# One-bank sums in the input phase and a new order of block products in the output phase of a fused attention and two-expert kernel

## The chip, the cores and the metric

The kernel runs on one core of one Trainium2 chip. The metric is the device time of one execution in microseconds (us); a lower time is better.

## The reference

Causal local attention with a few global keys feeds two dense blocks one after the other. The part that matters here is the last block, on 3072 tokens:

```python
x = _moe_ref(x=x, ...)          # (a * b @ w3) @ w_out, d_model 512
h = x @ w_in                    # 512 -> 2048
g = h * np.cos(h)
return (g @ w_out).astype(np.float32)   # 2048 -> 512
```

## The kernel before

Attention and the first block take the first 616 us of the span and are the same before and after. What follows handles the last block. The 3072 tokens go in three rounds (q = 0, 1, 2) of 1024, each in two blocks of 512 columns. A round has an input phase (h = x @ w_in, and g = h cos h) and an output phase (g @ w_out).

Both phases use a scheme with seven block products in place of eight. Every product of fp32 matrices is made of three fp32r matmuls (`mm3`, L419): each operand is split into a high part and a low remainder, and high x high, high x low and low x high are summed in a PSUM bank.

**Input phase** (`phase_a`, L1141, called for k = 0 to 7): one call makes a pair of 128-row blocks of h, as tiles `jj` and `gg` of 128x1024. It issues seven products (`prod`, L1065) of six matmuls each, in the order 0 to 6 of the list `PRODS`, so 42 matmuls of 128x512. They go to four sums a, b, c, d: product 0 starts a, 1 starts b, 2 starts c, 3 starts d, then 4 is added to a, 5 to c, 6 to d. In between, the sums are read as partial results: ACT copies a (`s1`, L1162), VectorE (DVE) makes `s` = b + s1, `v` = c + s (written to tile `vv`), and `gg`'s second half = d + v (all L1152); once 4, 5 and 6 have been added, ACT copies a into `jj` (L1188), and DVE writes c + s to `gg` and d + s to `jj`. Before the change a and b are the two halves of one PSUM tile of two banks, and c and d those of another (`two_banks`, L1062), from a ring of four such tiles, which is the whole PSUM.

A **gate** (class `Gate`, L1081) turns a finished tile h of 128x1024 into h cos h: `turns` (ACT, L1088, into a two-bank PSUM tile of integers), two fused multiply-adds (DVE, `rest_steps`, L1097), absolute value (`size`, ACT, L1103), sine (`cosine`, ACT, L1106), multiply (`times`, GpSimd, here POOL, L1111). The gates of k - 1 are spread over the call for k, the tail of g0 over the call after that.

**Output phase** (`phase_b`, L1265): 56 steps, seven products times eight pairs k, in an order written out as the list `turn` (L1113). A step makes six matmuls, three into each of two banks. Its moving operand `op` is split by `op_split` (L1208): a copy to fp32r on ACT (L1214), a subtraction on DVE (L1215), three steps ahead of its use. Operands of products 1, 2, 3 and 6 are first made by `fold` (L1223), a subtraction, on POOL for 2 and 3 and on DVE for 1 and 6. The gates of pair 7 and the tail of those of pair 6 run inside the first steps (`last_gates`, L1235), since the input phase ends with pair 7. `evict` (L1287) adds finished sums up and sends them out.

Every engine runs its instructions in the order in which the code issues them. Weights come as `piece` tiles of 512 KB, loaded by the SP queue in the order of use (`pieces_to`, L1125) into a ring of eight; a load waits until the tile that it takes over has been read. `op` tiles rotate over two slots of tag `op` and four of tag `Wb`; the gates' work tiles `r` use `Wb` too. Remainders of the next round's input operands (`x2_steps`) run on ACT and DVE from step 16 on and in the first call of the next input phase. In round 0 three small steps of `needs_general` (L721) take turns with the steps of the output phase.

Of the kernel before, what the change touches and what calls it, by code (L numbers as in the profile page):

```python
# [271 lines left out]
def fused(ctx, tc, a_qk, a_v, a_v0, w3p, wo1p, w1p, w2p, winp, wo2p, out):  # L272
# [448 lines left out]
    def needs_general(nv, psum):  # L721

        misc.tile([128, 88], F32, name="fill_f")
        f = misc.tile([128, 4], F32, name="flags")
        nl, ng = nv[:, 0:1], nv[:, 1:2]
        nc.vector.tensor_reduce(
            out=f[:, 0:1], in_=top.rearrange("p a b -> p (a b)"), axis=AXIS.X, op=ALU.max
        )
        nc.vector.tensor_scalar(f[:, 0:1], f[:, 0:1], -0.9 * NEG, None, ALU.is_ge)
        nc.vector.tensor_scalar(f[:, 1:2], nl, 1.0, None, ALU.is_lt)  # L730
        nc.vector.tensor_scalar(f[:, 2:3], nl, float(LOC + 1), None, ALU.is_gt)
        nc.vector.tensor_scalar(f[:, 3:4], ng, float(GLB), None, ALU.is_gt)
        yield
        t = psum()[:, 0, :]
        nc.tensor.transpose(t[0:4, 0:128], f, ident)
        m = misc.tile([4, 128], F32, name="flag_rows")
        nc.vector.tensor_copy(out=m, in_=t[0:4, 0:128])
        c = misc.tile([4, 1], F32, name="flag_col")
        nc.vector.tensor_reduce(out=c, in_=m, axis=AXIS.X, op=ALU.max)
        yield  # L740
        nc.tensor.transpose(t[0:1, 128:132], c, ident[0:4, 0:4])
        r = misc.tile([1, 4], F32, name="flag_row")
        nc.vector.tensor_copy(out=r, in_=t[0:1, 128:132])
        flag = misc.tile([1, 1], F32, name="flag")
        nc.vector.tensor_reduce(out=flag, in_=r, axis=AXIS.X, op=ALU.max)
        flag_i = misc.tile([1, 1], I32, name="flag_i")
        nc.vector.tensor_copy(out=flag_i, in_=flag)
        yield flag_i

    with tc.manual_schedule():  # L750
# [309 lines left out]
        banks = {}  # L1060

        def two_banks(dt=F32):  # L1062
            return p_h.tile([128, 2, TB2], dt, tag="h", name="h_ps")

        def prod(q, k, i):  # L1065

            bank, name = PRODS[i]
            if i in (0, 2):
                t = two_banks()
                banks["ab" if i == 0 else "cd"] = t  # L1070
                for e in range(2):
                    banks["abcd"[i + e]] = t[:, e, :]
            n, half = divmod(7 * k + i, 2)
            w, x = pieces[q, n][:, half], x2c[name]
            mm3(
                banks[bank],
                [(w[:, e, 0, :], w[:, e, 1, :], x[:, e, 0, :], x[:, e, 1, :]) for e in range(2)],
                i < 4, True, i >= 4,
            )
# [34 lines left out]
        for prods, ks in (  # L1114
            ((0,), range(NP - 1)), ((2,), range(NP - 3)), ((0,), (NP - 1,)),
            ((2,), range(NP - 3, NP)), ((4, 1, 3, 5, 6), range(NP)),
        ):
            turn += [(i, k) for i in prods for k in ks]
# [22 lines left out]
        def phase_a(q, k, x2_last):  # L1141
# [27 lines left out]
            if k:  # L1169
                fold(3, k - 1)  # L1170
            if k > 1:
                fold(2, k - 2)
            prod(q, k, 2)
# [16 lines left out]
            add(gg[:, 0, :], banks["c"], s)  # L1190
            if k == NP - 1:
                for n in range(3):
                    op_split(0, n)
            g1[k].turns()
            add(jj[:, 1, :], banks["d"], s)

        t3 = {}
# [9 lines left out]

        def op_split(i, k):  # L1208
            at = op_count[0] % 6
# [4 lines left out]
            nc.scalar.copy(out=t[:, 0, :], in_=x)  # L1214
            nc.vector.tensor_tensor(  # L1215
                out=t[:, 1, :], in0=x, in1=t[:, 0, :].bitcast(F32), op=ALU.subtract
# [3 lines left out]

        def fold(i, k):

# [8 lines left out]
            }[i]  # L1231
            engine = nc.gpsimd if i in (2, 3) else nc.vector
            engine.tensor_tensor(out=out, in0=p, in1=q, op=ALU.subtract)  # L1233

        def last_gates():  # L1235
# [5 lines left out]
            a, b = g1[k].rest_steps(homes[0]), g0[k].rest_steps(homes[1])  # L1241
            next(a)
            g0[k - 1].cosine()
            g0[k - 1].times()
            yield
            next(a)
            g0[k].turns()
            fold(2, k - 1)
            yield
            next(b)  # L1250
            g1[k].size()
            g1[k].cosine()
            g1[k].times()
            yield
            next(b)
            yield
            g0[k].size()
            g0[k].cosine()
            g0[k].times()
            yield  # L1260
            fold(3, k)
            fold(2, k)
            yield

        def phase_b(q):  # L1265
# [21 lines left out]
            def evict(n):  # L1287

                p = ps[PRODS[n][0]]
                if n == 0:  # L1290
                    nc.scalar.copy(out=sv, in_=p)
                elif n == 2:
                    total(wv, p, sv)
                elif n == 4:
                    o = raw()
                    nc.scalar.copy(out=o, in_=p)
                    nc.sync.dma_start(out=place(0, 0), in_=o)
                elif n == 1:
                    total(sv, p, sv)
                    total(wv, p, wv)  # L1300
                elif n == 3:
                    total(wv, p, wv)
                    nc.sync.dma_start(out=place(1, 1), in_=wv)
                elif n == 5:
                    o = raw()
                    total(o, p, sv)
                    nc.sync.dma_start(out=place(0, 1), in_=o)
                elif not final:
                    total(sv, p, sv)
                    nc.sync.dma_start(out=place(1, 0), in_=sv)  # L1310

            def evict_last(i):

                for h, queue_ in enumerate((nc.scalar, nc.sync)):
                    c = slice(h * 256, h * 256 + 256)
                    total(sv[:, i, c], ps["d"][:, i, c], sv[:, i, c])
                    queue_.dma_start(out=place(1, 0)[:, i, c], in_=sv[:, i, c])

            def step(n, k, which):
# [3 lines left out]
                for i in which:  # L1323
                    if k == 0 and n < 4 and i == 0:
                        ps[bank] = two_banks()
                    mm3(
                        ps[bank][:, i, :],
                        [(w[:, i, 0, :], w[:, i, 1, :], x[:, 0, :], x[:, 1, :])],
# [3 lines left out]
            for at, (n, k) in enumerate(turn):  # L1332
                pieces_to(base + pairs_of.index((n, k // 2)) + 6)
                if at + 3 < len(turn):
                    op_split(*turn[at + 3])
                some(gates, 1)
                if at == 8 and not final:
                    x2_loads(q + 1)
# [5 lines left out]
                    x2_next = x2_steps(r0, r1)  # L1344
                for i, lag in ((1, 13), (6, 29)):
                    if 0 <= at - lag < NP:
                        fold(i, at - lag)
                if x2_next and at >= 16 and at % 3 == 0:
                    some(x2_next, 1)
                if q == 0 and at in (26, 30, 34):  # L1350
                    flags_of[0] = next(steps_f)
# [11 lines left out]

        steps_f = needs_general(nv, two_banks)
        flags_of = [None]
# [4 lines left out]
        flag = flags_of[0]  # L1370
        for p in (p_h, p2, late, x2cA, wts, edge):
            p.release()
# [85 lines left out]
```

## Time and profile before

| what | before |
|---|---|
| median of 3 runs (lowest to highest) | 1150.86 us (1150.82 to 1151.83) |
| the profiled execution: its own time, its span | 1149.4 us, 1147.2 us |
| PE matmul busy | 1087.0 us (95%) |
| DVE busy | 846.7 us (74%) |
| ACT busy | 728.3 us (63%) |
| POOL busy | 258.4 us (23%) |
| chain that ended last, by engine | PE 76%, DVE 15%, ACT 4% |

The span runs from the first to the last instruction that the profile shows, and 2.2 us of the execution lie around it. PE is the matrix engine and PEld its weight loads, which overlap the matmuls. A matmul's recorded duration contains the depth of the pipeline, so a row's duration is longer than the time until the next one starts; the pace is read from the starts. A bracket at the end of a timeline row is the engine's idle time before it and what ended that.

### The profile page before, as it was taken

The numbers are of one execution on the slowest core, as the hardware profiler recorded it, in microseconds if no ns is written. First come the engines' busy times: TensorE is split into PE (matmuls) and PEld (weight loads), VectorE is DVE, ScalarE is ACT, GpSimd is POOL, SyncE is SP. The second block draws the span as 40 slices with busy tenths as digits, with TensorE's granted clock in tenths as the row PEclk, the third lists the DMA queues.
The fourth block names the chain that finished last, engine by engine and source line by source line (L and its number), as shares of the span: only waits on it lengthen the run. The fifth ranks groups of instructions, "written<-read, shape, count | busy, mean of one in ns | idle before, by whom it ended". The sixth has DMA issues, their size and how long they took to land.

```text
span 1147.2 us, 17759 instructions
## 1 busy us (share of the span) xinstructions
PE 1087.0 (95%) x5922; PEld 928.3 (81%) x5922; DVE 846.7 (74%) x1807; ACT 728.3 (63%) x1475; POOL 258.4 (23%) x255
## 2 busy tenths in 40 slices
PE   8999999999999999999999888999898899988897
PEld 4557999999999999999998676777676687766585
DVE  8887768788687877878363677795767896777783
ACT  8988867676676776767332676463666553667541
POOL 0000011111121111112000666100566200466200
PEclk9999999999999999999999999899999999999999
DMA  9855466665766665674524455557554647545452
GB/s 334 277 180 170 146 206 200 223 211 186 233 201 227 206 218 194 208 229 138 187 98 138 165 176 174 182 193 265 168 164 163 211 174 275 170 164 164 144 183 95
DMA packets 88309, 219.25 MB, mean 191 GB/s; under 512 B 9488, under 2 KB 26384, under 8 KB 88208
## 3 DMA queue, kind: packets, MB, share of 16 engines
q1 hardware_dynamic: 87696, 217.44, 57.1%
q8 instruction: 49, 0.80, 0.3%
q10 hardware_dynamic: 512, 0.58, 0.2%
q14 instruction: 52, 0.43, 0.1%
HBM read 176.04 MB, written 41.94 MB: 190 GB/s over the span
## 4 chain that ended last, share of the span: by engine, by line
PE 76%; DVE 15%; ACT 4%; issue 2%; DMA 1%; POOL 0%; DVEq 0%; ACTq 0%; POOLq 0%; SPq 0%
PE h_ps L419 32%; PE mm L419 32%; DVE op L1215 3%; PE x_ps L644 3%; DVE r L1097 3%; PE mm L869 3%; PE pt_ps L617 2%; DVE gr L1152 1%; PE s_ps L559 1%; PE s_ps L555 1%; PE pt_ps L619 1%; ACT e L608 1%; DVE jj L1233 1%; PE s_ps L547 1%; ACT r L1103 1%
## 5 line engine op out<-in xcount | busy, mean ns | idle before, releaser
L419 PE MATMUL h_ps<-op,piece 128*128 128x512 f32 x1008 | 241.6, 398 | 20.3 <-DVE op L1215 16.1
L419 PEld LDWEIGHTS h_ps<-op,piece 128*128 128x128 f32 x1008 | 190.2, 191 | 70.6 <-DVE op L1215 24.8
L610 POOL TENSOR_SCALAR e<-e,st 128x232 f32<-128x232 f32 x148 | 77.0, 533 | 475.6 <-DVE st L602 388.7
L419 PE MATMUL mm<-xT,wA 128*128 128x384 f32 x768 | 146.7, 340 | 0.5 <-ACT xT L658 0.4
L419 PE MATMUL mm<-xT,wB 128*128 128x384 f32 x768 | 146.2, 339 | 0.0
L419 PE MATMUL mm<-ab,W 128*128 128x384 f32 x768 | 146.2, 340 | 0.0
L419 PE MATMUL h_ps<-B,piece 128*128 128x512 f32 x432 | 113.4, 397 | 26.6 <-DVE gr L1152 24.7
L419 PE MATMUL h_ps<-T,piece 128*128 128x512 f32 x576 | 138.4, 389 | 0.0
L419 PEld LDWEIGHTS mm<-xT,wA 128*128 128x128 f32 x768 | 130.9, 188 | 3.2 <-issue 1.8
L419 PEld LDWEIGHTS mm<-ab,W 128*128 128x128 f32 x768 | 131.1, 188 | 2.4 <-issue 2.4
L419 PEld LDWEIGHTS mm<-xT,wB 128*128 128x128 f32 x768 | 130.9, 188 | 2.1 <-issue 2.1
L419 PEld LDWEIGHTS h_ps<-T,piece 128*128 128x128 f32 x576 | 108.1, 188 | 22.7
L419 PEld LDWEIGHTS h_ps<-B,piece 128*128 128x128 f32 x432 | 79.1, 188 | 52.9 <-DVE gr L1152 33.6
L1111 POOL TENSOR_TENSOR gr<-r,gr 128x1024 f32<-128x1024 f32 x24 | 57.0, 2376 | 275.7 <-ACT r L1106 189.7
L589 ACT ACTIVATE e<-e,top 128x232 f32<-128x232 f32 (+1 forms) x192 | 89.3, 468 | 2.0 <-DVE top L578 2.0
L522 ACT CAST hh<-qk 128x720 fp32r<-128x720 f32 x74 | 58.9, 796 | 45.8 <-PE s_ps L559 43.1
L1103 ACT ACTIVATE r<-r 128x1024 f32<-128x1024 f32 x48 | 51.0, 1062 | 52.8 <-DVE r L1097 52.4
L578 DVE CUSTOM_DVE_ANT_0 e<-s_ps,bias 128x232 f32<-128x232 f32 (+1 forms) x192 | 65.0, 374 | 14.6 <-PE s_ps L559 9.7
L1111 POOL TENSOR_TENSOR jj<-r,jj 128x1024 f32<-128x1024 f32 x24 | 58.1, 2423 | 62.4 <-ACT r L1106 62.4
L1215 DVE TENSOR_TENSOR op<-jj,op 128x512 fp32r<-128x512 f32 x72 | 56.9, 810 | 14.8 <-ACT op L1214 14.8
L1215 DVE TENSOR_TENSOR op<-gr,op 128x512 fp32r<-128x512 f32 x72 | 57.6, 845 | 10.6 <-ACT op L1214 10.5
L869 PE MATMUL mm<-wo,w 128*128 128x512 f32 x128 | 61.2, 606 | 1.7 <-DVE wo L360 1.7
(129 smaller groups left out, 1860.8 us busy)
## 6 DMA issues: line engine op xcount, KB each, us to landing
piece<-a_s SPq DMA_DIRECT2D x84, 512.0 KB, 3.3
piece<-o2s SPq DMA_DIRECT2D x84, 512.0 KB, 3.3
qk<-in_a_qk SPq DMA_DIRECT2D x74, 360.0 KB, 3.4
a_s<-ap SPq DMA_DIRECT2D x56, 256.0 KB, 2.5
o2s<-ap SPq DMA_DIRECT2D x56, 256.0 KB, 2.4
v<-in_a_v SPq DMA_DIRECT2D x95, 128.0 KB, 3.3
raw<-in_w3p SPq DMA_DIRECT2D x16, 512.0 KB, 5.1
raw<-in_winp SPq DMA_DIRECT2D x16, 512.0 KB, 3.6
```

The costliest lines, as they stand in the source:

```text
L419: nc.tensor.matmul(ps, lhsT=l, rhs=r, start=first and i + e == 0, stop=last and i == n - 1 and e == 2, skip_group_check=more,)
L522: nc.scalar.copy(out=hh[n], in_=qk_raw[n])
L578: nc.vector.tensor_tensor_reduce(out=es[n][:, e, :w], in0=sp[:, e, :w], in1=bias[:, 2 * p + e, :], scale=-0.125, scalar=3.0e38, op0=ALU.ad ...
L589: nc.scalar.activation(es[n][:, e, :w], es[n][:, e, :w], ACTF.Exp, bias=top[:, n, e:e + 1], scale=-1.0, accum_out=sts[n][:, 0, e:e + 1],)
L610: nc.gpsimd.tensor_scalar(x, x, st[:, 1, e:e + 1], 1.0, ALU.mult, ALU.mult)
L617: nc.tensor.transpose(pt_ps[:, e, 0, :], e_t[:, e, :128], ident)
L644: nc.tensor.matmul(x[e * 64:(e + 1) * 64, i * 128:(i + 1) * 128], lhsT=vt[:kk, c, e * 64:(e + 1) * 64], rhs=pt[:kk, e, c, :], start=c == 0 ...
L869: nc.tensor.matmul(W_ps[m], lhsT=wt["w3", c][:, m * 128:(m + 1) * 128], rhs=wt["wo1", k], start=k == 0, stop=k == M1 - 1,)
L1097: nc.vector.scalar_tensor_tensor(out=self.r, in0=self.kt, scalar=-c, in1=x, op0=ALU.mult, op1=ALU.add)
L1103: nc.scalar.activation(self.r, self.r, ACTF.Abs)
L1111: nc.gpsimd.tensor_tensor(out=self.h, in0=self.r, in1=self.h, op=ALU.mult)
L1215: nc.vector.tensor_tensor(out=t[:, 1, :], in0=x, in1=t[:, 0, :].bitcast(F32), op=ALU.subtract)
```

## The change

The four sums of the input phase become four tiles of one bank each (pool `p_h`, four banks), and the remaining four banks are two tiles of two banks (pool `p_k`) for the gates' integers and for the output phase's sums b and c; its sums a and d take two one-bank tiles each. The output phase begins with products 0, 3 and 2 over pairs 0 to 6, then does pair 7 of these three, then products 4, 1, 5, 6 over all pairs; before it was product 0 over pairs 0 to 6, product 2 over 0 to 4, pair 7 of product 0, the rest of product 2, then 4, 1, 3, 5, 6. Operands are split four steps ahead instead of three; those of steps 0 and 1 are split during the calls for k = 6 and k = 7, with the subtraction on POOL, and those of steps 2 and 3 at the end of the call for k = 7. The last three folds of products 2 and 3 move from POOL to DVE, at steps 8, 10 and 12. The steps of `last_gates` are grouped anew. `evict` handles sums a and d by halves, and sum d is added when product 1 is done.

```diff
@@ -731,7 +731,7 @@
         nc.vector.tensor_scalar(f[:, 2:3], nl, float(LOC + 1), None, ALU.is_gt)
         nc.vector.tensor_scalar(f[:, 3:4], ng, float(GLB), None, ALU.is_gt)
         yield
-        t = psum()[:, 0, :]
+        t = psum()
         nc.tensor.transpose(t[0:4, 0:128], f, ident)
         m = misc.tile([4, 128], F32, name="flag_rows")
         nc.vector.tensor_copy(out=m, in_=t[0:4, 0:128])
@@ -1059,17 +1059,19 @@
         p_h = pool("p_h", 4, space=PSUM)
         banks = {}
 
+        p_k = pool("p_k", 2, space=PSUM)
+
+        def one_bank():
+            return p_h.tile([128, TB2], F32, tag="h", name="h_ps")
+
         def two_banks(dt=F32):
-            return p_h.tile([128, 2, TB2], dt, tag="h", name="h_ps")
+            return p_k.tile([128, 2, TB2], dt, tag="k", name="k_ps")
 
         def prod(q, k, i):
 
             bank, name = PRODS[i]
-            if i in (0, 2):
-                t = two_banks()
-                banks["ab" if i == 0 else "cd"] = t
-                for e in range(2):
-                    banks["abcd"[i + e]] = t[:, e, :]
+            if i < 4:
+                banks[bank] = one_bank()
...
@@ -1112,8 +1114,8 @@
 
         turn = []
         for prods, ks in (
-            ((0,), range(NP - 1)), ((2,), range(NP - 3)), ((0,), (NP - 1,)),
-            ((2,), range(NP - 3, NP)), ((4, 1, 3, 5, 6), range(NP)),
+            ((0, 3, 2), range(NP - 1)), ((0, 3, 2), range(NP - 1, NP)),
+            ((4, 1, 5, 6), range(NP)),
         ):
             turn += [(i, k) for i in prods for k in ks]
         pairs_of = list(dict.fromkeys((i, k // 2) for i, k in turn))
@@ -1167,9 +1169,11 @@
             gate(g1, k - 1, "cosine")
             gate(g1, k - 1, "times")
             if k:
-                fold(3, k - 1)
+                fold(3, k - 1, nc.gpsimd)
             if k > 1:
-                fold(2, k - 2)
+                fold(2, k - 2, nc.gpsimd)
+            if k >= NP - 2:
+                op_split(0, k - NP + 2, nc.gpsimd)
             prod(q, k, 2)
             prod(q, k, 3)
             some(x2_last, 2)
@@ -1188,11 +1192,11 @@
             nc.scalar.copy(out=jj[:, 0, :], in_=banks["a"])
             gate(g0, k - 1, "size")
             add(gg[:, 0, :], banks["c"], s)
-            if k == NP - 1:
-                for n in range(3):
-                    op_split(0, n)
             g1[k].turns()
             add(jj[:, 1, :], banks["d"], s)
+            if k == NP - 1:
+                op_split(0, 2)
+                op_split(0, 3)
 
         t3 = {}
 
@@ -1205,20 +1209,20 @@
 
         ops, op_count = {}, [0]
 
-        def op_split(i, k):
+        def op_split(i, k, engine=nc.vector):
             at = op_count[0] % 6
             op_count[0] += 1
             p, kw = (p2, {"tag": "op", "bufs": 2}) if at < 2 else (wts, {"tag": "Wb", "bufs": 4})
             t = ops[i, k] = p.tile([128, 2, TB2], F32R, name="op", **kw)
             x = raw_of(i, k)
             nc.scalar.copy(out=t[:, 0, :], in_=x)
-            nc.vector.tensor_tensor(
+            engine.tensor_tensor(
                 out=t[:, 1, :], in0=x, in1=t[:, 0, :].bitcast(F32), op=ALU.subtract
             )
 
         t3_two = {}
 
-        def fold(i, k):
+        def fold(i, k, engine=nc.vector):
 
             if i == 3:
                 if k % 2 == 0:
@@ -1229,7 +1233,6 @@
                 3: (t3.get(k), t[5], t[2]), 2: (t[2], t[2], t[0]),
                 1: (t[2], t[5], t[2]), 6: (t[4], t[4], t[2]),
             }[i]
-            engine = nc.gpsimd if i in (2, 3) else nc.vector
             engine.tensor_tensor(out=out, in0=p, in1=q, op=ALU.subtract)
 
         def last_gates():
@@ -1240,26 +1243,21 @@
             ]
             a, b = g1[k].rest_steps(homes[0]), g0[k].rest_steps(homes[1])
             next(a)
+            next(a)
             g0[k - 1].cosine()
             g0[k - 1].times()
             yield
-            next(a)
             g0[k].turns()
-            fold(2, k - 1)
-            yield
-            next(b)
             g1[k].size()
             g1[k].cosine()
             g1[k].times()
             yield
+            yield
             next(b)
-            yield
+            next(b)
             g0[k].size()
             g0[k].cosine()
             g0[k].times()
-            yield
-            fold(3, k)
-            fold(2, k)
             yield
 
         def phase_b(q):
@@ -1288,32 +1286,35 @@
 
                 p = ps[PRODS[n][0]]
                 if n == 0:
-                    nc.scalar.copy(out=sv, in_=p)
+                    for i in range(2):
+                        nc.scalar.copy(out=sv[:, i, :], in_=p[i])
                 elif n == 2:
                     total(wv, p, sv)
                 elif n == 4:
                     o = raw()
-                    nc.scalar.copy(out=o, in_=p)
+                    for i in range(2):
+                        nc.scalar.copy(out=o[:, i, :], in_=p[i])
                     nc.sync.dma_start(out=place(0, 0), in_=o)
                 elif n == 1:
                     total(sv, p, sv)
                     total(wv, p, wv)
-                elif n == 3:
-                    total(wv, p, wv)
+                    for i in range(2):
+                        total(wv[:, i, :], ps["d"][i], wv[:, i, :])
                     nc.sync.dma_start(out=place(1, 1), in_=wv)
                 elif n == 5:
                     o = raw()
                     total(o, p, sv)
                     nc.sync.dma_start(out=place(0, 1), in_=o)
-                elif not final:
-                    total(sv, p, sv)
+                elif n == 6 and not final:
+                    for i in range(2):
+                        total(sv[:, i, :], p[i], sv[:, i, :])
                     nc.sync.dma_start(out=place(1, 0), in_=sv)
 
             def evict_last(i):
 
                 for h, queue_ in enumerate((nc.scalar, nc.sync)):
                     c = slice(h * 256, h * 256 + 256)
-                    total(sv[:, i, c], ps["d"][:, i, c], sv[:, i, c])
+                    total(sv[:, i, c], ps["d"][i][:, c], sv[:, i, c])
                     queue_.dma_start(out=place(1, 0)[:, i, c], in_=sv[:, i, c])
 
             def step(n, k, which):
@@ -1322,18 +1323,24 @@
                 x = ops[n, k]
                 for i in which:
                     if k == 0 and n < 4 and i == 0:
-                        ps[bank] = two_banks()
+                        if bank in "ad":
+                            ps[bank] = [one_bank(), one_bank()]
+                        else:
+                            t = two_banks()
+                            ps[bank] = t
                     mm3(
-                        ps[bank][:, i, :],
+                        ps[bank][i] if bank in "ad" else ps[bank][:, i, :],
                         [(w[:, i, 0, :], w[:, i, 1, :], x[:, 0, :], x[:, 1, :])],
                         n < 4 and k == 0, k == NP - 1, n >= 4,
                     )
 
             for at, (n, k) in enumerate(turn):
                 pieces_to(base + pairs_of.index((n, k // 2)) + 6)
-                if at + 3 < len(turn):
-                    op_split(*turn[at + 3])
                 some(gates, 1)
+                if at + 4 < len(turn):
+                    op_split(*turn[at + 4])
+                if at in (8, 10, 12):
+                    fold(*{8: (2, NP - 2), 10: (3, NP - 1), 12: (2, NP - 1)}[at])
                 if at == 8 and not final:
                     x2_loads(q + 1)
                     r0, r1 = (
@@ -1342,12 +1349,12 @@
                     )
                     nc.sync.dma_start(out=r0, in_=x2_cols("B12", q + 1))
                     x2_next = x2_steps(r0, r1)
-                for i, lag in ((1, 13), (6, 29)):
+                for i, lag in ((1, 21), (6, 31)):
                     if 0 <= at - lag < NP:
                         fold(i, at - lag)
                 if x2_next and at >= 16 and at % 3 == 0:
                     some(x2_next, 1)
-                if q == 0 and at in (26, 30, 34):
+                if q == 0 and at in (34, 38, 42):
                     flags_of[0] = next(steps_f)
                 if final and at >= len(turn) - 4:
                     if at == len(turn) - 1:
@@ -1361,14 +1368,14 @@
                         evict(n)
             return x2_next
 
-        steps_f = needs_general(nv, two_banks)
+        steps_f = needs_general(nv, one_bank)
         flags_of = [None]
         for q in range(NQ):
             for k in range(NP):
                 phase_a(q, k, x2_now)
             x2_now = phase_b(q)
         flag = flags_of[0]
-        for p in (p_h, p2, late, x2cA, wts, edge):
+        for p in (p_k, p_h, p2, late, x2cA, wts, edge):
             p.release()
```

## Rows read from the trace of the kernel before

**Rows 1.** Windows: the six phases of three rounds; columns in the first line.

```profile
core 0: us, PE busy (x) PEld busy (x) DVE busy (x) ACT busy (x) POOL busy (x), PEclk, DMA share, GB/s
...
615.69:702.61 86.92, 78.69 (x337) 62.43 (x337) 58.41 (x67) 54.58 (x61) 46.77 (x26) 1.00 0.54 178
702.61:790.40 87.79, 81.56 (x339) 64.97 (x339) 72.71 (x101) 45.56 (x69) 13.24 (x7) 0.96 0.60 204
790.40:878.05 87.65, 78.77 (x337) 62.33 (x336) 61.89 (x70) 54.35 (x61) 46.74 (x26) 1.00 0.55 180
878.05:965.04 86.99, 80.57 (x337) 63.24 (x337) 72.01 (x91) 45.56 (x69) 13.05 (x7) 0.98 0.60 206
965.04:1052.71 87.67, 78.79 (x338) 62.33 (x336) 61.88 (x70) 54.34 (x61) 46.71 (x26) 1.00 0.54 180
1052.71:1139.40 86.69, 79.05 (x337) 62.38 (x336) 63.55 (x85) 41.39 (x64) 13.23 (x7) 1.00 0.44 149
```

**Rows 2.** Waits of PE, 615 to 1147 us: in total, times, longest.

```profile
PE h_ps L419 <- DVE gr L1152: 24.7, 23, 1.2
PE h_ps L419 <- DVE op L1215: 16.1, 12, 2.0
```

**Rows 3.** Timeline, one call of the input phase: start, us, engine, line, [idle before].

```profile
846.50 4.24 PE L419 MATMUL h_ps<-T,piece 128*128 128x512 f32 x18
...
850.58 1.52 PE L419 MATMUL h_ps<-B,piece 128*128 128x512 f32 x6
850.78 0.69 DVE L1152 TENSOR_TENSOR vv<-h_ps,sv 128x512 f32<-128x512 f32 x1 [0.50 <-PE h_ps L419]
...
852.52 0.68 DVE L1152 TENSOR_TENSOR gr<-h_ps,vv 128x512 f32<-128x512 f32 x1
...
853.26 1.66 PE L419 MATMUL h_ps<-B,piece 128*128 128x512 f32 x6 [1.15 <-DVE gr L1152]
...
854.75 1.53 PE L419 MATMUL h_ps<-T,piece 128*128 128x512 f32 x6
...
856.32 0.69 DVE L1152 TENSOR_TENSOR gr<-h_ps,sv 128x512 f32<-128x512 f32 x1 [1.98 <-PE h_ps L419]
```

**Rows 4.** Timeline of PE, first call of an input phase after an output phase.

```profile
798.64 1.43 PE L419 MATMUL h_ps<-B,piece 128*128 128x512 f32 x5 [0.57 <-DVE B L948]
```

**Rows 5.** Lines, 660 to 1147 us: count, busy us, mean ns, idle before.

```profile
L1111 POOL TENSOR_TENSOR jj<-r,jj 128x1024 f32<-128x1024 f32 x22 | 53.3, 2424 | 58.0 <-ACT r L1106 58.0
L1097 DVE SCALAR_TENSOR_TENSOR r<-h_ps,r 128x1024 f32<-128x1024 int32 x42 | 51.1, 1217 | 0.6
...
L1106 ACT ACTIVATE r<-r,half_pi 128x1024 f32<-128x1024 f32 x43 | 49.3, 1146 | 0.8
L1103 ACT ACTIVATE r<-r 128x1024 f32<-128x1024 f32 x42 | 44.6, 1062 | 48.4 <-DVE r L1097 48.1
...
L1233 POOL TENSOR_TENSOR gr<-gr,jj 128x512 f32<-128x512 f32 x22 | 30.4, 1383 | 0.5
...
L1215 DVE TENSOR_TENSOR op<-t,op 128x512 fp32r<-128x512 f32 x24 | 16.3, 680 | 0.2
...
L1214 ACT CAST op<-t 128x512 fp32r<-128x512 f32 x24 | 14.9, 622 | 13.6 <-PE h_ps L419 11.4 <-DVE op L1215 2.2
```

**Rows 6.** Timeline, output phase of round 2, a multiply on POOL and a split.

```profile
889.32 2.35 POOL L1111 TENSOR_TENSOR gr<-r,gr 128x1024 f32<-128x1024 f32 x1 [2.33 <-ACT r L1106]
...
889.78 2.44 DVE L1215 TENSOR_TENSOR op<-jj,op 128x512 fp32r<-128x512 f32 x1 [1.08 <-ACT op L1214]
...
892.27 4.71 PE L419 MATMUL h_ps<-op,piece 128*128 128x512 f32 x12 [1.98 <-DVE op L1215]
```

**Rows 7.** Timeline of PE, output phase of round 3, end of its early waits.

```profile
1072.30 63.32 PE L419 MATMUL h_ps<-op,piece 128*128 128x512 f32 x275 [1.99 <-DVE op L1215]
```

**Rows 8.** Timeline of ACT, output phase of round 2, an operand's copy.

```profile
881.12 0.62 ACT L1214 CAST op<-jj 128x512 fp32r<-128x512 f32 x1 [1.12 <-PE h_ps L419]
```

**Rows 9.** The page's DMA issues: KB each, median us to landing.

```profile
piece<-o2s SPq DMA_DIRECT2D x84, 512.0 KB, 3.3
```

## The prediction

> **What bounds it now.** I first cut the span into its phases [rows 1]. From 615.7 us on PE is the engine to shorten, but not by its arithmetic: 18 matmuls start within 846.50 to 850.58 [rows 3], so the pace is 4.08/18 = 0.2267 us, and a phase of 8 x 42 = 336 matmuls (both kinds) needs 76.2 us. The input phases take 86.9, 87.7 and 87.7 us, the output phases 87.8, 87.0 and 86.7. About 11 us of each phase is PE standing still. Then I read PE's waits [rows 2]: they have two causes, DVE's writes of `gg` in the input phase (23 times, at most 1.2 us) and operand splits in the output phase (12 times, up to 2.0 us).
>
> The timeline of one input call shows the first [rows 3]. Product 4 starts at 850.58, product 5 should follow 1.36 later at 851.94 and starts at 853.26; 0.13 more is lost refilling, as product 6 follows after 1.49. That is 1.45 per call. It waits for the write of `gg` that reads sum d (852.52 to 853.20), though it adds to c, whose last reader `vv` ended at 851.47: waits go by the two-bank tile. So does the read of c at 856.32, which sits until product 6 (into d) has ended.
>
> **The input phase after it.** With a tile per bank product 5 waits for `vv` alone, and product 6 for the write that reads d. Is DVE ready? I count from the start of product 0. The read of c no longer waits for product 6 and ends at -0.5 instead of +0.9. `turns` follows to 0.55 (some 1.06 on ACT, like its neighbours), then two fused steps of 1.22 to 3.35, `s` to 4.0, `vv` to 4.6, a fused step to 5.8, the write of `gg` to 6.4 [rows 3, 5]. Product 5 starts at 6.80 and product 6 at 8.16, so there is 1.7 us to spare. Loads per call against 42 x 0.2267 = 9.52: DVE 4 x 1.22 + 5 x 0.68 = 8.3; ACT 2 x (1.06 + 1.06 + 1.15) + 2 x 0.62 = 7.8; POOL 2 x 2.42 + 2 x 1.38 = 7.6. No engine takes PE's place. The seven calls k = 1 to 7 lose their 1.45 each, and k = 0 its smaller wait. In rounds 2 and 3 the remainder of an operand (B22) is still late at k = 0 [rows 4]; by the same order of DVE's work it costs about 0.5 instead of 1.3. So: 76.2 + 76.7 + 76.7 = 229.6 against 86.92 + 87.65 + 87.67 = 262.2, a gain of 32.6.
>
> A page would give more: the Trainium skill, TensorE: Matmul & The Clock Gate, in "A second HAM failure mode: psum-queue depth-cycling", has short idles between groups of matmuls toggle the clock. This trace disagrees for this phase, whose granted clock is 1.00 in all three rounds with a wait in every call [rows 1]. Were it right, a clock as low as the 0.96 of the first output phase would be worth another 4% of 262, some 10 us; I count nothing.
>
> **The output phase after it.** Before, 49 matmuls stand between 1052.71 and 1072.30 [rows 1, 7]: 19.6 us for 11.1 us of work. The 8.5 us lost is pair 7's gates running on ACT, DVE and POOL among the operand splits. The new order needs pair 7 at step 21, not 12, but the splits of the early steps still stand behind the gates on the engines. What costs most is visible in [rows 6]: a split on DVE, two SBUF inputs, 0.68 us by itself [rows 5], takes 2.44 since it cannot proceed until POOL's multiply (889.32 to 891.67) ends. I take this as one at a time, first come. DVE's sums and fused steps, which read PSUM, run their usual times beside POOL.
>
> Time 0 is the end of product 6 of k = 7; delays accumulate.
> - POOL ends its two folds at 1.1 and the remainder for step 1 at 2.4 (no row shows this form; the fold of 128x512, 1.38, is nearest; bounds 0.68 and 2.42). Step 1 wants it at 1.6: **0.85**.
> - ACT: `turns` to 0.6, copies for steps 2 and 3 to 1.7, sine of pair 6's g0 to 2.8; POOL multiplies 2.9 to 5.4. DVE's split for step 2 (after POOL) ends 3.1, for step 3 behind the multiply 6.1: **0.83**. Then two fused steps to 8.4 and the split for step 4 at 9.0: **1.47**.
> - ACT: size of g1 8.5 to 9.6, sine to 10.7, and only then the copy for step 5, to 11.2: **0.96** for the high part. POOL's multiply runs 10.8 to 13.2, so the split ends at 13.9: **2.26**.
> - g0 repeats it: split 6, two fused steps to 16.8, split for step 7 (product 3, pair 0): **0.71**; sine to 19.1, copy for step 8: **0.96**; multiply to 21.6, split at 22.3: **2.26**.
>
> The sum is 10.3, with 8 refills of 0.13 11.3: 87.5 in round 3. In rounds 1 and 2 the eviction after product 1 now makes two totals and two half totals on DVE (2 x 1.22 + 2 x 0.68) among splits and the next round's `x2_steps`: 0.9 near the end, so 88.4 in round 1. In round 2 the slots fall otherwise: the copy for step 3 must wait for step 0 (before, that wait for PE is at 881.12 [rows 8]); this puts the sine later and lets DVE's split go first: 86.1. Together 262.0 against 261.5, and 0.5 for the clock, which fell to a mean of 0.96 in round 1 and 0.98 in round 2 in such a stretch [rows 1] and may again. Output phases: 1 us longer.
>
> **Edits at nothing.** The three folds moved to DVE at steps 8, 10, 12 (0.68 each) lie where each step gives DVE 1.36 and the split takes 0.68; uncovered, 2 us a round. Halved copies and totals: under 0.2 us each, behind later steps; uncovered 0.4. The flags, moved to steps 34 to 42, want a one-bank tile only after product 4 has freed one. SP: pieces (0,3), (3,3), (2,3) now stay longer in the ring of eight, yet by steps of first and last use every load is still issued at least eight steps (11 us) ahead, against 3.3 us to land [rows 9].
>
> **Sum.** 1149.4 - 32.6 + 1.0 = 1117.8 for the profiled execution (span 1147.2 and 2.2 around it); the median lies 1.5 above that execution, so I forecast 1119. Bounds: POOL's remainder 3 us either way over three rounds; one more or one fewer split caught behind a multiply 2.3 per round, 7 either way; slack misjudged by 0.3 per call, 6 worse. The likeliest case's own range is 1112 to 1128.
>
> **Rivals.**
> - *The early output phase is covered* (10%): the order gives pair 7 nine more steps. If steps 5 and 8 find their operands ready, 2 x 3.2 per round go, 19 us: 1100. Against it stands that their copies are issued behind a sine on ACT.
> - *The early output phase gets worse* (8%): the copies run four steps ahead and each stands behind more gate work; one more wait like the 1.0 + 2.3 per round: 1129.
> - *The wait stays in the input phase, in part* (4%): DVE is late for product 6 instead, half of the 1.45 is left: 1134. *The tiles bring nothing* (2%), since product 6 waits for the same write as product 5 did: 1151. Against both, 1.7 us of slack.
> - *Slower* (3%): PE's clock falls. If PE worked at the lower level, 1.2 GHz, from the first early wait on, each matmul would take 0.45 us; to lose the 32 us of the input phases, each output phase must run some 47 matmuls so on top of its waits (3 x 47 x 0.2267). At 62 it is 1161. It decides where the clock stays low beyond the last early wait. For it: 0.96 and 0.98 in two rounds; against it: 1.00 in the third with the same waits [rows 1]. The page named above, section "HAM oscillation — how this bites in real kernels", has idle stretches drop the clock to half; here two rounds of three agree.
>
> **How the numbers follow.** The forecast has 73%. Faster and slower count beyond 0.2% of 1150.86, 2.3 us, about what a measurement of this kernel can tell. All cases but two are faster, 0.95; no change 0.02; slower 0.03. With 1112 to 1128 holding 73%, 1108 to 1131 takes in half of the neighbouring cases and leaves out some 2 in 10.
>
> **What would show it.** In the profile after: the waits of PE for `gg` gone, calls of the input phase 9.5 us apart instead of 10.98, DVE idle less. In the output phase waits for operands at steps 1, 3, 4, 5, 7 and 8, with 2 us ones under POOL's multiplies, and none later than about 23 us in. I am wrong if input calls stay over 10 us apart, or if an output phase falls under 84 or goes over 91 us.

## The result, and the profile after

The changed kernel takes 1122.49 us (median of 4, 1120.62 to 1123.45) against 1150.84 before: a ratio of 0.9752, 95% interval 0.9735 to 0.977. The profiled execution took 1121.77 us, with a span of 1120.0. The forecast was 1119 us, with a range of 1108 to 1131.

The windows of the six phases after, which answer to [rows 1]:

```profile
615.35:691.55 76.20, 76.20 (x337) 63.07 (x337) 58.99 (x68) 56.02 (x63) 47.90 (x27) 1.00 0.60 202
691.55:783.68 92.13, 83.69 (x339) 65.73 (x338) 74.41 (x103) 45.67 (x70) 9.63 (x5) 0.93 0.56 194
783.68:860.47 76.79, 76.46 (x338) 63.01 (x336) 62.16 (x72) 55.23 (x62) 47.91 (x27) 1.00 0.61 205
860.47:949.55 89.08, 81.80 (x338) 65.49 (x336) 70.89 (x93) 45.76 (x70) 9.72 (x5) 0.94 0.59 202
949.55:1026.33 76.78, 76.45 (x337) 63.00 (x336) 62.24 (x72) 55.21 (x62) 47.65 (x26) 1.00 0.62 205
1026.33:1113.90 87.57, 80.43 (x337) 64.53 (x335) 62.62 (x86) 41.22 (x65) 10.67 (x6) 0.96 0.44 149
```

The first number behind each window is its length. The input phases fell from 262.2 to 229.8 us together, 32.5 less. The output phases rose from 261.5 to 268.8, 7.3 more. The stretch before the first phase is 0.3 shorter and the one after the last matmul 1.7 shorter: together the 27.2 by which the span shrank.

PE's waits after, from 600 us on, which answer to [rows 2] (us in total, times, longest):

```profile
PE h_ps L419 <- DVE op L1219: 13.2, 8, 2.0
PE h_ps L419 <- ACT op L1218: 5.5, 6, 1.6
PE h_ps L419 <- POOL op L1219: 3.0, 3, 1.4
PE k_ps L419 <- DVE op L1219: 1.2, 2, 0.9
PE h_ps L419 <- DVE B L948: 0.7, 2, 0.3
```

The 24.7 us for `gg` are gone, and nothing replaced them in the input phase but 0.3 us each in two rounds for the late remainder of B22. One call in the timeline, beside [rows 3]:

```profile
1022.25 2.88 PE L419 MATMUL h_ps<-B,piece 128*128 128x512 f32 x12
...
1022.76 2.41 POOL L1113 TENSOR_TENSOR gr<-r,gr 128x1024 f32<-128x1024 f32 x1 [1.11 <-ACT r L1108]
1022.83 0.68 DVE L1154 TENSOR_TENSOR gr<-h_ps,vv 128x512 f32<-128x512 f32 x1
...
1024.97 1.52 PE L419 MATMUL h_ps<-T,piece 128*128 128x512 f32 x6
1025.17 0.69 DVE L1154 TENSOR_TENSOR gr<-h_ps,sv 128x512 f32<-128x512 f32 x1 [0.53 <-PE h_ps L419]
```

Products 4 and 5 are one run of 12 matmuls, and product 6 follows 2.72 us after the first of them, which is 12 x 0.2267. `gg`'s write from sum d ends at 1023.51, 1.46 us before product 6 starts. The read of c begins at 1025.17, 0.20 after product 6 has started, so it no longer waits for product 6 to end.

The early output phase of round 3 in the timeline (start, us, engine, line, idle before):

```profile
1027.50 2.53 DVE L1219 TENSOR_TENSOR op<-jj,op 128x512 fp32r<-128x512 f32 x2 [0.28 <-ACT op L1218]
1027.75 1.73 POOL L1219 TENSOR_TENSOR op<-jj,op 128x512 fp32r<-128x512 f32 x1
...
1029.53 5.51 PE L419 MATMUL h_ps<-op,piece 128*128 128x512 f32 x23 [1.45 <-POOL op L1219]
...
1034.78 2.35 POOL L1113 TENSOR_TENSOR gr<-r,gr 128x1024 f32<-128x1024 f32 x1 [2.48 <-ACT r L1108]
1035.24 3.04 DVE L1219 TENSOR_TENSOR op<-jj,op 128x512 fp32r<-128x512 f32 x2 [2.22 <-ACT op L1218]
...
1035.26 0.51 PE L419 MATMUL h_ps<-op,piece 128*128 128x512 f32 x1 [0.22 <-ACT op L1218]
...
1037.73 4.25 PE L419 MATMUL h_ps<-op,piece 128*128 128x512 f32 x11 [1.97 <-DVE op L1219]
...
1043.02 2.35 POOL L1113 TENSOR_TENSOR jj<-r,jj 128x1024 f32<-128x1024 f32 x1 [5.89 <-ACT r L1108]
...
1043.50 0.50 PE L419 MATMUL h_ps<-op,piece 128*128 128x512 f32 x1 [1.52 <-ACT op L1218]
...
1045.97 6.21 PE L419 MATMUL h_ps<-op,piece 128*128 128x512 f32 x20 [1.98 <-DVE op L1219]
```

The pattern is the one forecast: step 1 waits for POOL's remainder, step 5 for ACT's copy behind a sine and then for DVE's subtraction behind POOL's multiply (1034.78 to 1037.13), and 12 matmuls on step 7 for the same again. The forecast had this second pair at step 8. New is how long the clock stays down. Windows of 2.5 us in round 1, after (behind the length: PE busy, PEld, DVE, ACT, POOL, granted clock):

```profile
700.00:702.50 2.50, 1.43 (x5) 0.86 (x5) 0.35 (x1) 2.47 (x4) 0.39 (x1) 1.00 0.58 202
702.50:705.00 2.50, 0.49 (x1) 0.19 (x1) 2.43 (x2) 0.56 (x2) 1.95 (x1) 0.84 0.00 0
705.00:707.50 2.50, 2.44 (x6) 1.96 (x7) 2.46 (x4) 0.00 (x0) 0.00 (x0) 0.50 0.00 0
...
717.50:720.00 2.50, 2.50 (x12) 2.01 (x11) 1.10 (x2) 0.99 (x2) 0.00 (x0) 0.93 0.30 71
```

The four windows left out, from 707.5 to 717.5, are at 0.50 too, that is 1.2 of 2.4 GHz. After the first two of these windows, in which 5 matmuls and 1 started, PE runs at half speed for about 14 us. Before, in round 1, it fell too, twice, and was back within 4 us each time; the first:

```profile
717.50:720.00 2.50, 2.50 (x8) 1.96 (x7) 0.30 (x1) 2.47 (x4) 0.76 (x1) 0.57 1.00 339
720.00:722.50 2.50, 0.70 (x3) 0.28 (x2) 2.50 (x2) 2.08 (x5) 2.50 (x2) 1.00 0.54 209
```

### The profile page after: what moved, and what is told of

It reads as the page before. It is cut to its first block, busy times and chain, and to the rows that moved or that the text cites. A ratio compares the mean times of both kernels' runs of the same rounds, so it can differ in the third digit from the quotient of the medians.

```text
span 1120.0 us, 17799 instructions
## 1 busy us (share of the span) xinstructions
PE 1085.7 (97%) x5922; PEld 936.3 (84%) x5922; DVE 848.0 (76%) x1815; ACT 730.7 (65%) x1481; POOL 251.2 (22%) x252
## 4 chain that ended last, share of the span: by engine, by line
PE 50%; DVE 7%; ACT 2%; issue 1%; POOL 0%; DVEq 0%; POOLq 0%
PE h_ps L419 29%; PE mm L419 12%; PE k_ps L419 6%; DVE op L1219 3%; DVE r L1099 1%; PE x_ps L644 1%; DVE jj L1236 1%; ACT r L1105 1%; ACT op L1218 1%; PE pt_ps L617 0%; DVE res L1278 0%; ACT r L1108 0%; PE s_ps L559 0%; PE s_ps L555 0%; PE pt_ps L619 0%
## 5 line engine op out<-in xcount | busy, mean ns | idle before, releaser
L419 PE MATMUL h_ps<-op,piece 128*128 128x512 f32 x576 | 148.8, 416 | 21.7 <-DVE op L1219 13.2
L419 PEld LDWEIGHTS h_ps<-op,piece 128*128 128x128 f32 x576 | 115.0, 202 | 53.6 <-DVE op L1219 16.3
L419 PE MATMUL h_ps<-B,piece 128*128 128x512 f32 x432 | 106.3, 390 | 0.7 <-DVE B L948 0.7
L419 PE MATMUL k_ps<-op,piece 128*128 128x512 f32 x432 | 100.5, 390 | 1.2 <-DVE op L1219 1.2
L419 PEld LDWEIGHTS k_ps<-op,piece 128*128 128x128 f32 x432 | 80.8, 188 | 18.9 <-DVE op L1219 2.0
L1218 ACT CAST op<-gr 128x512 fp32r<-128x512 f32 x72 | 44.0, 623 | 43.4 <-PE k_ps L419 15.0
L1219 DVE TENSOR_TENSOR op<-jj,op 128x512 fp32r<-128x512 f32 x66 | 54.6, 849 | 17.5 <-ACT op L1218 17.5
```

The lines of the kernel that those rows point to most:

```text
L419: nc.tensor.matmul(ps, lhsT=l, rhs=r, start=first and i + e == 0, stop=last and i == n - 1 and e == 2, skip_group_check=more,)
L1219: engine.tensor_tensor(out=t[:, 1, :], in0=x, in1=t[:, 0, :].bitcast(F32), op=ALU.subtract)
```

## The experiments

**Tiles alone.** One-bank sums, with the output phase's order, lead, splits, folds and gates of before (its sums a and c take one-bank pairs and are evicted by halves):

```diff
             if i < 4:
                 banks[bank] = one_bank()
...
-                        ps[bank] = two_banks()
+                        ps[bank] = [one_bank(), one_bank()] if bank in "ac" else two_banks()
```

> One-bank sums alone, with the output phase's order, splits, folds and gates as before (its sums a and c take one-bank pairs, b and d two-bank tiles). Theory: the whole gain is PE's wait in the input phase, so input phases take 76.2, 76.8 and 76.8 us and output phases 87 to 89 as before; 1118 to 1122 us, no slower than the changed kernel. Rival: the new order of the output phase carries part of the gain; then output phases stay as before while the changed kernel's would have to be shorter, and this one is 5 us or more slower than the changed kernel.

Measured: 1118.23 us (ratio to before 0.9716, 0.9699 to 0.9732). Input phases 76.2, 76.8, 76.8. The output phases in its windows:

```profile
691.20:777.99 86.79, 81.47 (x339) 64.34 (x339) 73.36 (x102) 45.98 (x71) 13.66 (x7) 0.96 0.60 207
...
854.82:944.06 89.24, 81.62 (x338) 64.67 (x337) 72.64 (x92) 45.99 (x71) 13.19 (x7) 0.96 0.60 201
...
1020.89:1108.70 87.81, 81.15 (x337) 64.68 (x336) 64.26 (x86) 41.84 (x66) 13.63 (x7) 0.96 0.44 148
```

The output phases are 2.4 us longer together than before, two of them 0.2 outside the 87 to 89 expected. The tiles carry the whole gain; the rest of the change costs some 4 us (1122.49 against 1118.23), the intervals of the two ratios just apart. In the profiles the difference is round 1, 92.13 against 86.79: PE waits 8.5 us there in the changed kernel and 5.2 in this one, at a clock of 0.93 and 0.96.

**Order alone.** The changed kernel with the two-bank tiles of before:

```diff
-            if i < 4:
-                banks[bank] = one_bank()
+            if i in (0, 2):
+                t = two_banks()
+                banks["ab" if i == 0 else "cd"] = t
...
```

> The new order, lead of four, early splits and folds on DVE alone, with the two-bank tiles of before. Theory: input phases stay near 87 us, output phases 87 to 92, so 1150 to 1160 us, not faster than before. Rival: the order gains by itself; under 1146 us.

Measured: 1156.70 us, ratio 1.0048 (1.0031 to 1.0065). PE's wait in the input phase is as in [rows 2]:

```profile
PE h_ps L419 <- DVE gr L1152: 24.7, 23, 1.2
```

Input phases are 86.9, 87.6 and 87.6, output phases 90.6, 89.1 and 89.6, 269.3 together against 268.8 in the changed kernel. The order by itself is half a percent slower, and the theory holds.

**Early multiplies on DVE.** The changed kernel with `times` of `last_gates` on DVE:

```diff
-            g0[k - 1].times()
+            g0[k - 1].times(nc.vector)
...
-            g1[k].times()
+            g1[k].times(nc.vector)
...
-            g0[k].times()
+            g0[k].times(nc.vector)
```

> The changed kernel with the three multiplies of the early output phase on DVE instead of POOL. Theory: the 2 us waits at steps 5 and 8 are DVE's subtraction held up by POOL's multiply; on DVE a multiply takes 1.2 us and holds up the next subtraction by that much only. The 1.98 us waits shrink to about 1, output phases to 83 to 87 us, the whole to 1104 to 1112 us. Rival: the copies behind the sine on ACT decide, or the clock; then output phases stay at 87 to 92 us and the whole at 1119 to 1125.

Measured: 1112.54 us (0.9666, 0.965 to 0.9682), output phases 87.2, 86.0 and 86.3: the upper edge, 0.2 us outside in round 1 and half a microsecond for the whole. The longest wait for a subtraction fell from 2.0 to 0.9, as expected. But step 7 now waits 3.0 us for the copy alone:

```profile
PE h_ps L419 <- DVE op L1219: 5.9, 9, 0.9
```

```profile
1028.76 2.79 PE L419 MATMUL h_ps<-op,piece 128*128 128x512 f32 x11 [0.74 <-DVE op L1219]
...
1032.82 1.15 ACT L1108 ACTIVATE r<-r,half_pi 128x1024 f32<-128x1024 f32 x1
1033.87 3.20 ACT L1218 CAST op<-t 128x512 fp32r<-128x512 f32 x6
...
1034.53 0.79 PE L419 MATMUL h_ps<-op,piece 128*128 128x512 f32 x1 [2.98 <-ACT op L1218]
```

So the multiply was one of two causes in series. The other is the chain of two fused steps, size and sine, with six copies queued on ACT behind it. In the changed kernel that copy is as late: from the start of step 5's second matmul to step 7 there are 5.77 us in both (1028.76 to 1034.53 here, 1037.73 to 1043.50 there). There the 11 matmuls in between took 4.25 us, at a lower clock, and here 2.79; the slower ones only covered more of the wait.

**Splits ahead of the gate work**, the changed kernel with two statements in the other order:

```diff
-                some(gates, 1)
                 if at + 4 < len(turn):
                     op_split(*turn[at + 4])
+                some(gates, 1)
```

> The changed kernel with each operand split issued ahead of that step's gate work instead of behind it. Theory (the split of a step is held up by the multiply wherever it stands): the same waits come one step later, at steps 6 and 9, output phases change by less than 1.5 us each, 1118 to 1124 us. Rival: ACT's order is the cause; the 0.8 to 1.5 us waits for ACT's copies go, twice a round, and the whole falls to 1113 to 1116 us.

Measured: 1123.07 us; output phases 91.3, 88.6 and 90.1, PE's waits for ACT 5.1 us in place of 5.5. The pairs of waits stand one step later, at steps 6 and 8 instead of 5 and 7 in round 3, and are about as long: one step of lead by itself changes nothing. Round 3 is 2.6 longer and thus outside the 1.5, at a clock of 0.94 instead of 0.96.

**Both**, in one kernel:

```diff
-            g0[k - 1].times()
+            g0[k - 1].times(nc.vector)
...
-                some(gates, 1)
                 if at + 4 < len(turn):
                     op_split(*turn[at + 4])
+                some(gates, 1)
```

> Splits ahead of gate work, and the early multiplies on DVE, but the gate work still in the changed kernel's bunches. Theory: the chain of two fused steps, size and sine in one bunch still holds the copy issued behind it, so a wait near 3 us stays once per round at the second gate; output phases 84 to 87 us, the whole 1106 to 1112 us. Rival: either edit lacked the other, and both together clear the waits: under 1100 us.

Measured: 1110.65 us; output phases 86.6, 85.3 and 85.9, all within what was expected, and still three waits of 3.0 us for ACT's copies. The bunches remain the bound.

**The two early subtractions on DVE**, undoing one part of the change:

```diff
-                op_split(0, k - NP + 2, nc.gpsimd)
+                op_split(0, k - NP + 2)
```

> The changed kernel with the two early subtractions, in the calls for k = 6 and 7, on DVE instead of POOL. Theory: DVE must then wait there for POOL's multiply, and the sums behind it are late for products 5 and 6; the input phases grow by 4 to 7 us, while step 1's wait (3.0 us over three rounds) goes: 1130 to 1140 us. Rival: POOL's subtraction is only a cost; input phases stay at 76 to 77 us and the whole falls by 2 to 3 us, to 1119 or 1120.

Measured: 1142.30 us (0.9921, 0.99 to 0.9942). The theory's direction, by more than its numbers: input phases grew by 8.0 to 8.5 us, of which the wait shown first is 4.9 a phase. Waits of PE, and the call for k = 7 in round 3:

```profile
PE h_ps L419 <- DVE vv L1154: 14.7, 6, 3.2
```

```profile
1038.51 2.36 POOL L1113 TENSOR_TENSOR gr<-r,gr 128x1024 f32<-128x1024 f32 x1 [1.79 <-ACT r L1108]
1038.98 2.44 DVE L1219 TENSOR_TENSOR op<-jj,op 128x512 fp32r<-128x512 f32 x1 [2.29 <-ACT op L1218]
...
1041.35 0.68 DVE L1154 TENSOR_TENSOR vv<-h_ps,sv 128x512 f32<-128x512 f32 x1
...
1042.08 2.16 PE L419 MATMUL h_ps<-B,piece 128*128 128x512 f32 x6 [2.30 <-DVE vv L1154]
```

The subtraction is held by the multiply, and `vv`, which reads PSUM and would not be, stands behind it on DVE; product 5 waits for `vv`. Step 1's wait is gone, but the clock now falls in the input phases as well (0.98, 0.96, 0.96). POOL's two subtractions earn their place.

**The gate work spread out.** The changed kernel with pair 7's gates one piece at a time over steps 0 to 13, multiplies on DVE, folds at steps 14 to 16, each step's split ahead of its gate work, and the load of an operand for the next round (B12) at step 14 instead of 8:

```diff
-            next(a)
-            next(a)
             g0[k - 1].cosine()
-            g0[k - 1].times()
+            g0[k - 1].times(nc.vector)
+            yield
             yield
             g0[k].turns()
+            yield
+            next(a)
+            yield
+            yield
+            next(a)
+            yield
             g1[k].size()
+            yield
             g1[k].cosine()
...
-                some(gates, 1)
                 if at + 4 < len(turn):
                     op_split(*turn[at + 4])
-                if at in (8, 10, 12):
...
+                some(gates, 1)
+                if at in (14, 15, 16):
...
+                if at == 14 and not final:
...
```

> The changed kernel with pair 7's gate work spread over steps 0 to 13, one piece at a time and behind that step's operand split, its multiplies on DVE, and the three folds at steps 14 to 16. Theory: the early waits come from gate work in bunches, which hold copies behind a size and a sine and subtractions behind a multiply; with 21 steps before pair 7 is needed it fits between the splits. PE's waits in the early output phase nearly vanish but for step 1, the clock stays at 1.00, output phases take 78 to 82 us, the whole 1089 to 1099 us. Rival: the engines are simply full there, so the waits move to later steps; output phases stay over 85 us and the whole over 1108.

Measured: **1089.86 us** (median of 5), ratio 0.9468 (0.9452 to 0.9485). Its output phases and PE's longest waits:

```profile
691.75:771.92 80.17, 77.33 (x339) 62.91 (x338) 71.12 (x106) 44.35 (x70) 2.44 (x2) 1.00 0.64 224
...
848.71:927.31 78.60, 76.75 (x337) 62.91 (x336) 69.73 (x96) 44.62 (x70) 2.45 (x2) 1.00 0.64 228
...
1004.11:1081.90 77.79, 76.49 (x337) 62.81 (x335) 61.47 (x89) 40.40 (x65) 2.99 (x2) 1.00 0.49 167
```

```profile
PE k_ps L419 <- DVE op L1219: 2.5, 2, 1.4
PE h_ps L419 <- POOL op L1219: 1.5, 2, 0.8
```

The early waits but step 1's are gone (1.3 us of that one in round 3 stand under POOL's queue), and the clock is at 1.00 throughout. This kernel is faster than both the one before and the changed one.

**The same with the multiplies on POOL.** Against the kernel just shown:

```diff
-            g0[k - 1].times(nc.vector)
+            g0[k - 1].times(nc.gpsimd)
...
```

> The same spreading with the multiplies left on POOL. Theory (a multiply on POOL holds up DVE's next subtraction for up to 2.4 us, but with the four steps of lead most of that is covered): output phases 80 to 85 us, the whole 1094 to 1106 us, 3 to 8 us more than with the multiplies on DVE. Rival: which engine multiplies makes no difference once the work is spread; within 2 us of the kernel with DVE multiplies.

Measured: 1098.13 us; output phases 83.1, 81.9 and 79.2, clock 1.00. PE's waits for splits moved to later steps (products that write two-bank tiles):

```profile
PE k_ps L419 <- DVE op L1219: 7.1, 5, 1.8
```

The engine is worth 8.3 us, a little over the range; the spreading, with the splits ahead and the later folds and load that go with it, is worth 24 us (1122.49 against 1098.13). Of these the splits ahead alone brought nothing (1123.07); the folds and the load were not tried by themselves.

**Spreading within the old order.** The kernel with tiles alone, gate work spread over steps 0 to 8, multiplies and the three folds on DVE (the steps of `last_gates`, shortened):

```diff
+            g0[k - 1].cosine()
+            g0[k - 1].times(nc.vector)
+            yield
+            g0[k].turns()
+            next(a)
+            yield
+            next(a)
+            yield
+            g1[k].size()
+            yield
...
+            fold(2, k - 1)
+            yield
+            fold(3, k)
+            yield
+            fold(2, k)
+            yield
```

> One-bank sums, the output order of before with its lead of three, and the gate work spread as far as that order lets it: one piece a step over steps 0 to 8, multiplies on DVE, the three folds on DVE at steps 9 to 11, splits ahead of gate work. Theory: spreading removes the waits only with room, and pair 7 is wanted here from step 12 (its split at step 9), not step 21; some of the waits stay, output phases 81 to 86 us, the whole 1099 to 1111 us, so the new order is what makes room. Rival: the room of the old order is enough once the work is spread; within 4 us of the spread kernel with the new order (1089.9).

```profile
691.15:775.49 84.34, 80.26 (x339) 62.34 (x339) 72.08 (x108) 45.34 (x71) 1.17 (x1) 1.00 0.63 213
...
852.31:936.97 84.66, 80.37 (x338) 62.13 (x338) 70.86 (x98) 45.32 (x71) 1.16 (x1) 1.00 0.61 212
...
1013.82:1097.48 83.66, 79.39 (x337) 62.28 (x336) 63.05 (x92) 41.13 (x66) 1.17 (x1) 1.00 0.46 155
```

```profile
PE h_ps L419 <- DVE op L1217: 8.3, 16, 1.3
PE h_ps L419 <- ACT op L1216: 2.6, 3, 0.9
```

Measured: 1108.06 us, its output phases and PE's longest waits above: 10 us less than the tiles alone. The clock stays up here as well, but the waits remain: 18 us more than in the new order. The new order, with its lead of four and its early splits, does make room; the changed kernel leaves it unused. Which of the three makes it was not separated.

## Why the prediction was right, point by point

- **Input phases: right, to 0.2 us.** Forecast 76.2, 76.7 and 76.7; measured 76.20, 76.79 and 76.78. The tiles alone, and the order alone, show that this is the tiles' doing. The slack of 1.7 us before product 6 was 1.46, and 0.5 for the late B22 was 0.6.
- **The early output phase: the places right, the terms mis-sized.** Step 1, a pair of waits at step 5, and in round 1 steps 3 and 4 waited as listed. The second pair came at step 7 and not at 8: I had g0's size and sine issued one step after its fused steps, and the code issues all four at step 3; so its single wait of 0.71 went too. The expectations of the experiments repeat that slip. The forecast waits sum to 10.3 us a round and 0.9 later; measured are 22.9 us over three rounds (the first four rows of PE's waits after), 7.6 each.
- **Who comes first differs by round.** In round 1 POOL's multiply (694.33) was ahead of DVE's subtraction for step 3, which took 2.89 us, as forecast. In rounds 2 and 3 that subtraction came first, and steps 3 and 4 did not wait; the forecast had this for round 2 alone. In round 3 DVE's subtraction for step 2 (1027.50) was also ahead of POOL's remainder for step 1, which took 1.73 us instead of 1.27 and 1.28, and step 1 waited 1.45 us instead of 0.75. POOL had ended its folds 1.47 us into that phase, and 1.22 into the others; whether that decided the turn was not tried.
- **The term that was mis-sized most is the half microsecond "for the clock".** A phase is 76.2 us plus waits, plus a refill for each wait, plus the clock's deficit. With my 0.13 for a refill, round 1 leaves 92.13 - 76.2 - 8.5 - 1.0 = 6.4 for the clock, round 2 89.08 - 76.2 - 7.3 - 0.8 = 4.8, round 3 87.57 - 76.2 - 7.1 - 0.7 = 3.6, about 15 us in all. But the refill was mis-sized too: between 1035.26 and 1037.73 lie one matmul of 0.23 us, a wait of 1.97 and thus 0.27. With 0.27 for each of the 19 waits the clock's deficit is some 12 us, where I had 0.5 in all: I built the phases from 76.2 us and waits at the full clock, though 4% and 2% of the first two of before [rows 1] are 5.2 us already. Waits and refills were forecast at 33.4 us and come to 28.0. I had waits too long and the clock too short, and the two errors left 6.3 us in the output phases (268.8 against 262.5).
- **The two errors hang together.** In round 1 the 11 matmuls before step 7 took 5.06 us and the wait behind them 0.71; in round 3 it was 4.25 and 1.52, and with the multiplies on DVE 2.79 and 2.98. The sum is 5.77 each time: the operand's chain sets step 7's start, and there a lower clock only shortens the wait. What the clock costs by itself is therefore less than its 12 us, and no run measures it.

```profile
705.06 5.06 PE L419 MATMUL h_ps<-op,piece 128*128 128x512 f32 x11 [1.98 <-DVE op L1219]
710.83 0.80 PE L419 MATMUL h_ps<-op,piece 128*128 128x512 f32 x1 [0.71 <-ACT op L1218]
```

- **One sign of being wrong came true.** An output phase over 91 us was to show it, and round 1 took 92.13: there the account of the early output phase failed, on the clock. Two things in the total are luck. Round 3's 87.57 against 87.5 has 7.1 us of waits where 10.3 were forecast, and a fallen clock in place of the rest. And the forecast is only 4 us low because 2.4 us went that no term of it has: 0.3 ahead of the first phase, 0.4 around the span, and 1.7 after the last matmul. That last stretch is 6.1 us, and 6.2 in the spread kernel, where sum d has a tile per bank, and 7.8 before, 8.0 with tiles alone and 7.6 with the order alone, where it has not; why was not looked into.
- **The one-at-a-time rule for POOL and DVE: right.** Taking the multiply off POOL ended the 2.0 us waits; putting subtractions beside POOL's multiplies cost 8 us a phase, the clock included. The Trainium skill, SBUF — State Buffer, "Who interferes with whom", says that a VectorE instruction with two SBUF inputs contends with a GpSimd one that reads SBUF, while one with at most one SBUF input does not. These runs agree: 2.44 us for a subtraction beside a multiply, 0.68 for `gg`'s write from PSUM right after the multiply's start at 1022.76.
- **Edits at nothing: right.** No wait for the folds, the halved copies, the flags or a `piece` shows in the waits of PE.
- **The rivals.** Of the slower one, a falling clock, the mechanism came and took some 12 us, more than a quarter of its price of 42. The covered early phase did not come with this change, but the spread kernel shows that it was to be had: 32.6 us below the changed kernel, more than the 19 I priced; its clock stayed at 1.00, and in round 1 the waits at steps 3 and 4 went as well.

## What to carry to other kernels

Where one PSUM tile holds several sums, look at what a matmul waits for: if it is a reader of the other half, give each sum a tile of its own. Where a dependent chain (fused steps, size, sine, multiply) shares its engines with operands that PE needs at every step, issue it one piece per step, and give it the steps first. Cost an early wait twice, once by itself and once by the clock that it may take down; but where the next operand is late anyway, a lower clock before it costs nothing.

## What the runs showed of the hardware that was not expected

The clock differs between patterns with like waits. In the input phase of before PE idles 1.15 us in every call of 10.97 at a clock of 1.00 [rows 1, 3]; in round 1 after, waits of 1.34, 0.76 and 1.98 us with five matmuls and one between them brought 0.50, and it stayed so for 14 us, through waits of 0.71 and 1.69. In the spread kernels waits of up to 1.8 us, each alone, left it at 1.00. The Trainium skill, TensorE: Matmul & The Clock Gate, "HAM oscillation — how this bites in real kernels", has waits for DMA between bursts of matmuls drop the clock to half; the changed kernel's round 1 agrees in the half clock (0.50), though its waits are for split operands. The section behind it, "A second HAM failure mode: psum-queue depth-cycling", has frequent short idles between groups of matmuls make the clock swing; the input phase of before does not show that (1.00). Why much the same waits kept 1.00 in round 3 of before and gave 0.96 with tiles alone was not tried.
